# Two attention layers and two MLPs, forward and backward: the second turn's transposes, a row's transposition, the first V gradient blocks and the last stores in another order

## The chip, the cores and the metric

The kernel runs on one core of a Trainium2 chip. The metric is the time of one execution on the device, in microseconds (us); lower is better. The core has a matrix engine (PE, TensorE; its weight loads are shown apart as PEld), a vector engine (DVE), a scalar engine (ACT), a general engine (POOL, GpSimd) and a sync engine (SP), which here does nothing but issue DMA transfers. Sixteen DMA engines move the data between the chip's memory and the on-chip buffers. Each engine works through its own instructions in order; between engines there are semaphores, which the compiler's framework places from the reads and writes of each tile.

## The reference

A layer is a decode attention over a cache and a channel MLP, each behind a LayerNorm and with a residual; the same weights are used twice. The batch is 2, one token each, width 1024, 32 query heads over 4 key/value heads, 16,384 cached positions of 128 values, MLP width 3584, all in bf16.

```python
def _A_ref(x, k_cache, v_cache, wq, wo):
    q = (x @ wq).reshape(B, Sq, Hq, Dh).transpose(0, 2, 1, 3)
    k = jnp.repeat(k_cache, rep, axis=1)
    v = jnp.repeat(v_cache, rep, axis=1)
    p = _softmax(jnp.einsum("bhqd,bhkd->bhqk", q, k) * (Dh ** -0.5))
    o = jnp.einsum("bhqk,bhkd->bhqd", p, v)
    return o.transpose(0, 2, 1, 3).reshape(B, Sq, Hq * Dh) @ wo
def _B_ref(x, w1, b1, w2, b2):
    h = _gelu(_layernorm(x) @ w1 + b1)
    return h @ w2 + b2
x = x + _A_ref(_layernorm(x), ...); x = x + _B_ref(x, ...)   # layer 0
x = x + _A_ref(_layernorm(x), ...); x = x + _B_ref(x, ...)   # layer 1
```

What is returned is x and, by `jax.vjp` with a given gradient of x, the gradients of the input, the two caches (each 2 x 4 x 16384 x 128), Wq, Wo, W1, b1, W2 and b2: ten outputs, out_0 (x) to out_9.

## The kernel before, in words

Everything large passes through on-chip slots of 128 partitions x 4096 bf16 values (1 MB): sixteen slot tiles, and parts of tiles named e, ds and late at times when those are free. A quarter of one head's cache of one batch, a slab of Wq, Wo, W1 or W2, a transposed slab, or a block of a gradient on its way out, takes a slot (or half of one).

**The planner.** The code first lists pieces of work with `emit(fn, uses)` and only then runs them, in that very order (`Program`, L58 to L180). A piece names the chunks that it uses. `run` gives each chunk a slot as one comes free; the loads are issued on SP in the order of first use, so SP's queue is one line: a load that has to wait until its slot is free holds up every load behind it. `keep` looks for a chunk that is used again later: where the slots have room between the two uses, it stays and is not loaded again. The order on each engine is thus the order of the pieces, written by hand through lists, step numbers and the interleaving in the loops.

**The stages**, by the trace of before: attention forward of layer 0 to about 215 us, its MLP to 250, attention forward of layer 1 (`attn_fwd(1)`) to 413, the *second turn* to 448, attention backward of layer 1 (`attn_bwd(1)`) to 641, the turn to layer 0 to about 664, attention backward of layer 0 with all the weight and cache gradients beside it to 1097, and the last stores to 1107.9. A step of `attn_bwd` takes a quarter of a V chunk: a transpose on DVE (L537, 128 x 512 viewed as int32), eight products (L550), eight with K (L575), and small works hung on step numbers.

**The second turn** (L1447 to L1482). The residual xA of the second attention goes through a LayerNorm (`ln_fwd`, L623 to L645, called by `mlp_in`, L913): sums over partitions by PE (`part_sum`, L594) and short DVE operations that wait for each other. Then the products with W1 (`w1_fwd`, L854, matmuls at L862: eight chunks of W1, 28 products each), the gelu with its slope (L881 to L910), and, for the backward pass, the products with W1 transposed. For these each W1 chunk is turned on DVE (`turn_cols`, L470, instruction at L473): four column groups cg for each of eight chunks j, 32 turns. Chunks 0 to 3 make the first half and 4 to 7 the second; in each half, group cg of all four chunks lands in one turned chunk `w1t[half][cg]`, and there are eight of these. Each is read by 28 products (`turned_products`, L479, matmuls at L487). Besides, a slab of Wo is turned on PE and copied by ACT for the next pass (`wo_first_ops`, `turn_here`, L452 and L455; eight "wo turns" of eight 128 x 128 transposes). Before, four W1 turns lie behind `attn_fwd(1)`, twenty beside the W1 products with four wo turns, one in the middle of the gelu with the other four wo turns, and seven behind it; then all eight groups of products. `mlp_in_bwd` (L918) takes the products back through the LayerNorm; from there gA_all (L932) goes through Wo (L465), and attention backward starts.

**The row to an output** (`col_to_row`, L609). x and the input's gradient lie as columns, 128 partitions x 8 groups x 2 batches, in f32. Eight PE transposes (L617), 128 x 2 to 2 x 128 each, and two DVE copies (L618) make two rows of 1024 values in bf16, which a DMA (L619) stores. For out_0 this happens at step 30 of `attn_bwd(1)` (L1507), in a half slot, and the DMA is issued by POOL; for out_1 near the end, by SP.

**The gradients of the caches** (`kv_outputs`, L1197). For each group pos of `attn_bwd(0)`, four chunks c and both w (1: V, 0: K) fill a block of 1 MB with eight units (L1261 products of 512 columns, copied out by `cast_out`, L276 on ACT or L279 on DVE). With `fine` (L1234), the units take the two halves of the block one after the other, and each half is stored as soon as it is full (L1267 to L1269); without, one store of 1 MB by POOL follows the eighth unit (L1271). Before, `fine` holds for the last group's K blocks from c = 2 on.

**The end** (L1158 to L1161 and `pieces_rows`, L1335). What is left behind the last step is a list `todo`; `parts` are the pieces that end in out_1's row, `kv_units` the last cache units, `units` the last of a weight gradient, out_4, whose eight stores of 256 KB (L1349) SP issues.

Of the kernel before, what the change touches and what calls it, by code (L numbers as in the profile page):

```python
# [182 lines left out]
def kernel(  # L183
# [24 lines left out]
    nc = tc.nc  # L208
# [400 lines left out]
    def col_to_row(colT, dram_out, queue=None, kind="half"):  # L609
        c = P.chunk(kind=kind)  # L610

        def f():
            row = c.ap[0:2, 0:D]
            for j0 in range(0, DJ, 4):
                ps = ob()[0:2, :].rearrange("p (a b) -> p a b", a=4)
                for j in range(4):
                    PE.transpose(ps[:, j, :], colT[:, j0 + j, :], identf[:])  # L617
                V.tensor_copy(out=row[:, j0 * 128:(j0 + 4) * 128], in_=flat(ps))  # L618
            (queue or GP).dma_start(dram_out, row)  # L619

        return f, [c]

    def ln_fwd(xT, name, twice=False):  # L623
        s1 = small.tile([128, 2], F32, name="ln_s1")
        V.tensor_reduce(out=s1[:], in_=xT.rearrange("p j b -> p b j"), axis=AX.X, op=ALU.add)
        ps = part_sum(s1[:], 2)
        negmu = small.tile([128, 2], F32, name="ln_negmu")
        V.tensor_scalar(out=negmu[:], in0=ps, scalar1=-1.0 / D, scalar2=None, op0=ALU.mult)
        xc = wrk.tile([128, DJ, 2], F32, name="ln_xc")
        V.tensor_tensor(out=xc[:], in0=xT, in1=bcast_j(negmu[:], DJ), op=ALU.add)  # L630
        sq = wrk.tile([128, DJ, 2], F32, name="ln_sq")
        V.tensor_tensor(out=sq[:], in0=xc[:], in1=xc[:], op=ALU.mult)
        s2 = small.tile([128, 2], F32, name="ln_s2")
        V.tensor_reduce(out=s2[:], in_=sq[:].rearrange("p j b -> p b j"), axis=AX.X, op=ALU.add)
        ps2 = part_sum(s2[:], 2)
        vpe = small.tile([128, 2], F32, name="ln_vpe")
        V.tensor_scalar(out=vpe[:], in0=ps2, scalar1=1.0 / D, scalar2=LN_EPS, op0=ALU.mult, op1=ALU.add)
        if twice:
            V.scalar_tensor_tensor(out=vpe[:], in0=vpe[:], scalar=LN_EPS, in1=vpe[:], op0=ALU.mult, op1=ALU.add)
            V.tensor_scalar(out=vpe[:], in0=vpe[:], scalar1=-LN_EPS, scalar2=None, op0=ALU.add)  # L640
        rstd = vec.tile([128, 2], F32, name=name + "_rstd")
        GP.tensor_tensor(out=rstd[:], in0=vpe[:], in1=neghalf[:], op=ALU.pow)  # L642
        y = vec.tile([128, DJ, 2], F32, name=name + "_y")
        V.tensor_tensor(out=y[:], in0=xc[:], in1=bcast_j(rstd[:], DJ), op=ALU.mult)
        return y, rstd  # L645
# [264 lines left out]
        V.tensor_tensor(out=h_all[:, :, 2 * l:2 * l + 2], in0=sg[:], in1=hpre[:], op=ALU.mult)  # L910
        return slope() if dh is None else None

    def mlp_in(l, xT):  # L913
        y, r = ln_fwd(xT[:], f"m{l}", twice=True)
        V.tensor_copy(out=m_all[:, :, 2 * l:2 * l + 2], in_=y[:])
        saved[f"m{l}"] = (y, r)

# [109 lines left out]
    def attn_bwd(l, order, gT, wo_first, outputs=None, mark=None, extra=None):  # L1027
# [127 lines left out]
        if l == 1:  # L1155
            todo = tail + parts
        else:
            rows, kv_units, units = outputs(s, True)  # L1158
            todo = ev.pop(s) + kv_units[0:4] + rows + kv_units[4:6] + tail[0:4] + kv_units[6:8] + tail[4:] + kv_units[8:10]
            todo += parts[0:1] + units[0:4] + parts[1:2] + units[4:8] + parts[2:3] + kv_units[10:13] + parts[3:]  # L1160
            todo += kv_units[13:] + units[8:]  # L1161
        for b in todo:
            emit(*b)
        assert not ev and not wb and not pend and not extra, (ev, wb, extra)
# [32 lines left out]
    def kv_outputs(pos, g):  # L1197
# [30 lines left out]
        for c, w in [(c, w) for c in range(NCH) for w in (1, 0)]:  # L1228
            at_ = base + 4 * c + 4 * (pos == 0) if w == 1 else base + 14 + 4 * c
            if w == 0 and pos == G - 1:  # L1230
                at_ = (124, 127, N_END + 1, N_END + 2)[c]
            stg = P.chunk(kind="full")
            hold = {}
            fine = w == 0 and pos == G - 1 and c > 1  # L1234

            def turn(c=c, w=w, hold=hold):
                st["tp"] += 1
                tp = tpb[st["tp"] % 2][:].bitcast(BF16)[:, 0:512].rearrange("p (a b) -> p a b", b=128)
                for bi in range(4):
                    for l in range(2):  # L1240
                        src = d_of(l, pos, g) if w == 0 else e_of(l, g)
                        PE.transpose(tp[64 * l:64 * l + 64, bi, :],  # L1242
                                     src[:, 4 * c + bi].rearrange("p h b -> p (h b)"), ident[:])
                st["blk"] += 1
                blk = Bt[st["blk"] % 3]
                src = tp.rearrange("p a (j t) -> p a j t", j=4)
                dst = blk[:].rearrange("p j (a t) -> p a j t", a=4)
                if st["act"] + 0.36 <= st["dve"] + 0.4:
                    S.copy(out=dst.bitcast(I32), in_=src.bitcast(I32))
                    load_of("act", 0.36)  # L1250
                else:
                    V.tensor_copy(out=dst, in_=src)
                    dve(0.4)
                hold["blk"] = blk

            res.append((min(at_ - 2, N_END - 1), turn, ()))
            for u in range(8):
                def unit(c=c, w=w, u=u, hold=hold, stg=stg, fine=fine):
                    ps = ob()
                    j, hf = (u % 4, u // 4) if fine else (u // 2, u % 2)  # L1260
                    PE.matmul(ps, lhsT=hold["blk"][:, j, :],  # L1261
                              rhs=flat(qm(w)[:, hf * 4:hf * 4 + 4, :]), start=True, stop=True)
                    cast_out(stg.ap.rearrange("p (s j q d) -> p s q j d", j=4, q=2, d=128)[
                        :, hf * 2:hf * 2 + 2, :, j], ps.rearrange("p (s q d) -> p s q d", q=2, d=128))
                    if fine:
                        if j == 3:
                            (nc.sync if w == 0 else GP).dma_start(  # L1267
                                (dKv if w == 0 else dVv)[g, :, c * 32 + hf * 16:c * 32 + hf * 16 + 16, :],
                                stg.ap[:, hf * 2048:hf * 2048 + 2048].rearrange("p (t d) -> p t d", d=128))  # L1269
                    elif u == 7:  # L1270
                        GP.dma_start((dKv if w == 0 else dVv)[g, :, c * 32:(c + 1) * 32, :],  # L1271
                                     stg.ap.rearrange("p (t d) -> p t d", d=128))
                res.append((at_ + (u // 4 if pos or w == 0 else u // 3), unit, [stg, qc]))
# [61 lines left out]
    def pieces_rows(out_ap, n_in, n_out, c0=0, fine=False):  # L1335
# [6 lines left out]
        for j0, rb, cb, cn in parts:  # L1342
            units = [(j0 + j, c0 + cb + c, 512, j * cn + c) for j in range(rb) for c in range(0, cn, 512)]

            def store(ap, n, j0=j0, rb=rb, cb=cb, cn=cn, end=len(units) - 1):
                if fine:
                    if n % 2 == 1:
                        j = n // 2
                        nc.sync.dma_start(out_ap[(j0 + j) * 128:(j0 + j + 1) * 128, c0:c0 + cn], ap[:, j * cn:(j + 1) * cn])  # L1349
                elif n == end:  # L1350
                    GP.dma_start(out_ap[j0 * 128:(j0 + rb) * 128, c0 + cb:c0 + cb + cn].rearrange("(j p) n -> p j n", p=128),
                                 ap[:, 0:rb * cn].rearrange("p (j n) -> p j n", j=rb))
# [94 lines left out]
    ws1 = ld_w1()  # L1447
    w1t = [[P.chunk() for _ in range(4)] for _ in range(2)]

    def w1_turn(j, cgs=range(4)):  # L1450
        return [turn_cols(ws1[j], j % 4, w1t[j // 4][cg], cg) for cg in cgs]

    xA1 = attn_fwd(1, down, lambda: xM0, mark("e1"), w1_turn(0), tw[5][1] + tw[6][0] + tw[6][1] + [(dh_last_, ())])
    emit(lambda: mlp_in(1, xA1))
    hps1, w1_ops = w1_fwd(1, ws1)
    dm_1 = quads(at_sb0(224, 16))
    vh1, spread_h1 = spread(lambda: dh_all[:, :, 2:4], FJ, "vh")
    ws_o, wo_turns1, wo_prods = wo_first_ops(1, up[0] % HKV)
    for j in range(DJ):
        for b in w1_ops[j] + (w1_turn(j) if 1 <= j < 6 else []) + wo_turns1[2 * j - 10:2 * j - 8] * (j in (5, 6)):  # L1460
            emit(*b)

    def turn_round():

        def dh(nslope):
            V.tensor_tensor(out=dh_all[:, :, 2:4], in0=nslope[:], in1=dh_last[:], op=ALU.mult)
            spread_h1()

        gelu(1, hps1, dh, lambda: [fn() for fn, _ in w1_turn(6, (0,)) + wo_turns1[4:]])

    emit(turn_round, [ws1[6], w1t[1][0]] + ws_o)
    for cg in range(4):
        for b in (w1_turn(6, (cg,)) if cg else []) + w1_turn(7, (cg,)):
            emit(*b)
    for h in range(2):
        for cg in range(4):
            for b in turned_products(lambda h=h: dm_1[:, h], w1t[h][cg], 14 * cg, 14, vh1, cg == 0, cg == 3):
                emit(*b)
    def g3_():
        saved["g3"] = mlp_in_bwd(1, lambda dm: unquad(dm[:].rearrange("p (c j) b -> p c j b", j=4), dm_1), gT4)  # L1480

# [156 lines left out]
```

## Time and profile before

| what | value |
|---|---|
| three runs, median (lowest to highest) | 1110.71 us (1108.69 to 1111.01) |
| the profiled execution: time, span of its instructions | 1109.68 us, 1107.9 us |
| PE, PEld, DVE, ACT, POOL busy | 810.2, 608.8, 761.4, 492.3, 178.5 us |
| mean granted PE clock | 0.929 |
| moved by DMA, mean rate | 450.03 MB, 406 GB/s |
| loads of V, of K (1 MB each) | 98, 105 |

All times in the profile count from the start of the span. The page gives the busy time of each engine, then the span in 40 equal slices with a digit for the busy share of each engine in tenths, the PE clock as granted, the share of the DMA engines and the rate. Groups of instructions are named by line, engine, operation and tile (out<-in). The timeline gives the start, the length, and the number of like instructions in a run ("x7"), whose ends may overlap; brackets tell how long the engine stood idle before and what released it. "SPq" and "POOLq" are the DMA issues of those engines. The waits list, for each line, what its engine waited for: total, times, longest.

### The profile page before, as it was taken

The numbers are of one execution on the slowest core, as the hardware profiler recorded it, in microseconds if no ns is written. First come the engines' busy times: TensorE is split into PE (matmuls) and PEld (weight loads), VectorE is DVE, ScalarE is ACT, GpSimd is POOL, SyncE is SP. The second block draws the span as 40 slices with busy tenths as digits, with TensorE's granted clock in tenths as the row PEclk, the third lists the DMA queues.
The fourth block names the chain that finished last, engine by engine and source line by source line (L and its number), as shares of the span: only waits on it lengthen the run. The fifth ranks groups of instructions, "written<-read, shape, count | busy, mean of one in ns | idle before, by whom it ended". The sixth has DMA issues, their size and how long they took to land. (4 is left out here: it accounts for less than half of the span.)

```text
span 1107.9 us, 34190 instructions
## 1 busy us (share of the span) xinstructions
PE 810.2 (73%) x14677; PEld 608.8 (55%) x14689; DVE 761.4 (69%) x1474; ACT 492.3 (44%) x1133; POOL 178.5 (16%) x571
## 2 busy tenths in 40 slices
PE   5664666457888647888678668878886987598795
PEld 4554565456777547777677565444443444344453
DVE  5864665169888627665646475979776896598984
ACT  0322223102233222235444326777675776477874
POOL 1000000001000000111111101433332332233430
PEclk9999999999999999999878657989996998799998
DMA  9999999999999998999999989999999999999996
GB/s 375 420 423 421 421 426 421 395 403 399 418 422 422 421 421 328 409 417 421 420 421 421 417 326 406 369 381 423 420 419 425 423 420 422 425 412 420 410 423 259
DMA packets 98312, 450.03 MB, mean 406 GB/s; under 512 B 7624, under 2 KB 11734, under 8 KB 59632
## 3 DMA queue, kind: packets, MB, share of 16 engines
q1 hardware_dynamic: 81232, 353.41, 78.4%
q0 software_dynamic: 16928, 94.43, 20.7%
q8 instruction: 115, 1.88, 0.6%
q14 instruction: 37, 0.30, 0.1%
HBM read 349.20 MB, written 98.62 MB: 404 GB/s over the span
## 5 line engine op out<-in xcount | busy, mean ns | idle before, releaser
L537 DVE STREAM_TRANSPOSE kT<-slot 128x512 int32<-128x512 int32 x420 | 283.2, 694 | 109.8 <-PE sc L550 89.5
L550 PE MATMUL sc<-qbd,kT 128*128 128x32 bf16 x4096 | 262.9, 223 | 11.0 <-DVE kT L537 9.7
L550 PEld LDWEIGHTS <-kT 128*128 128x128 bf16 x4096 | 209.3, 115 | 63.7 <-issue 33.6
L575 PEld LDWEIGHTS <-slot 128*128 128x128 bf16 x3520 | 144.0, 103 | 108.6 <-issue 45.0
L575 PE MATMUL sb<-xt,slot 128*128 128x8 bf16 x3520 | 161.3, 177 | 51.1 <-DMA slot<-in_A_v_cache_dram 24.5
L276 ACT CAST slot<-sc 128x512 bf16<-128x512 f32 x293 | 166.5, 594 | 57.1 <-PE sc L1321 32.6
L1261 PE MATMUL sc<-slot,late 128*128 128x512 bf16 x345 | 128.8, 393 | 19.0 <-DVE slot L279 6.5
L279 DVE CAST slot<-sc 128x512 bf16<-128x512 f32 x170 | 113.7, 677 | 25.1 <-PE sc L1261 13.4
L763 ACT ACTIVATE e<-sc 128x512 bf16<-128x512 f32 x32 | 19.0, 597 | 235.9 <-DVE sc L760 168.3
L276 ACT CAST slot<-sb 128x512 bf16<-128x512 f32 x139 | 82.4, 593 | 38.8 <-PE sb L1321 16.9
L455 ACT COPY slot<-tp 128x512 int32<-128x512 int32 x88 | 50.2, 586 | 105.5 <-PE tp L452 105.2
L452 PE MATMUL tp<-ident,slot 128*128 128x128 bf16 x768 | 71.3, 255 | 11.9 <-DMA slot<-in_A_wq_dram 6.2
L585 ACT COPY xt<-e 32x128 int32<-32x128 int32 x256 | 75.6, 295 | 3.9
L1261 PEld LDWEIGHTS <-late 128*128 128x128 bf16 x512 | 44.5, 98 | 59.6 <-issue 46.1
L1261 PE MATMUL sb<-slot,late 128*128 128x512 bf16 x161 | 63.6, 395 | 11.7 <-DVE slot L279 6.5
L1321 PE MATMUL sc<-slot,late 128*128 128x512 bf16 x157 | 60.5, 404 | 12.3 <-DVE e L279 6.9
L437 DVE STREAM_TRANSPOSE slot<-slot 128x1024 int32<-128x1024 int32 (+1 forms) x48 | 55.3, 1177 | 16.8 <-DMA slot<-in_A_wo_dram 8.5
L452 PEld LDWEIGHTS <-slot 128*128 128x128 bf16 x768 | 57.9, 116 | 14.5 <-DMA slot<-in_A_wq_dram 6.7
L279 DVE CAST slot<-sb 128x512 bf16<-128x512 f32 x82 | 55.6, 678 | 9.2 <-PE sb L1321 3.9
L642 POOL TENSOR_TENSOR m_rstd<-ln_vpe,neghalf 128x2 f32<-128x2 f32 x2 | 1.4, 717 | 352.6 <-DVE ln_vpe L640 352.6
L585 POOL COPY xt<-late 32x64 int32<-32x64 int32 x240 | 55.2, 230 | 12.9 <-DVE late L1049 2.2
L585 POOL COPY xt<-ds 32x64 int32<-32x64 int32 x128 | 29.5, 231 | 158.6 <-DVE ds L1049 115.3
(300 smaller groups left out, 1098.7 us busy)
## 6 DMA issues: line engine op xcount, KB each, us to landing
slot<-in_A_k_cache_dram SPq DMA_DIRECT2D x105, 1024.0 KB, 17.5
slot<-in_A_v_cache_dram SPq DMA_DIRECT2D x98, 1024.0 KB, 18.0
out_dram<-slot POOLq DMA_DIRECT2D x55, 1024.0 KB, 14.4
slot<-in_A_wq_dram SPq DMA_DIRECT2D x25, 1024.0 KB, 16.1
slot<-in_A_wo_dram SPq DMA_DIRECT2D x25, 1024.0 KB, 19.7
slot<-in_B_w_dram SPq DMA_DIRECT2D x23, 896.0 KB, 15.8
out_dram<-slot POOLq DMA_DIRECT2D x40, 512.0 KB, 14.3
slot<-in_B_w_dram SPq DMA_DIRECT2D x12, 1024.0 KB, 13.5
```

The costliest lines, as they stand in the source:

```text
L276: S.copy(out=dst, in_=src)
L279: V.tensor_copy(out=dst, in_=src)
L437: V.transpose(out=t.ap[:, h * nw * 256:(h + 1) * nw * 256].bitcast(I32).rearrange("p (w j m) -> p w j m", j=4, m=32), in_=c.ap[:, 0:4 * nc ...
L452: PE.transpose(tp[:, j * 128:(j + 1) * 128], c.ap[:, off + j * 128:off + (j + 1) * 128], ident[:])
L455: S.copy(out=d.bitcast(I32), in_=tp.bitcast(I32))
L537: V.transpose(out=kT[:].bitcast(I32).rearrange("p (w j m) -> p w j m", w=4, j=4), in_=c.ap[:, (i % 4) * 1024:(i % 4 + 1) * 1024].bitcast(I ...
L550: PE.matmul(sc[:, a0:a0 + 4, :, 2 * (i % 4) + q], lhsT=kv[:, 2 * q + w, :, e], rhs=qbd[:, q_at(g), 2 * w + e], start=(w == 0 and e == 0), ...
L575: PE.matmul(acc, lhsT=c.ap[:, n * 128:(n + 1) * 128], rhs=xv[:, i // 4, t // 2, :, 2 * (i % 4) + t % 2], start=(fresh and i == 0 and t == ...
L585: (GP.tensor_copy if on[t % len(on)] == "g" else S.copy)(out=d[32 * t:32 * t + 32, c0:c0 + cn, j, :], in_=s[32 * j:32 * j + 32, c0:c0 + cn ...
L763: S.activation(out=e_of(l, g)[:, 8 * f:8 * f + 8].rearrange("p a h b -> p h a b"), in_=sc[f][:].rearrange("p h (a b) -> p h a b", b=8), fu ...
L1261: PE.matmul(ps, lhsT=hold["blk"][:, j, :], rhs=flat(qm(w)[:, hf * 4:hf * 4 + 4, :]), start=True, stop=True)
L1321: PE.matmul(ps, lhsT=hold[j // 4 * 4][:, j % 4, :], rhs=Y.ap[:, y_at + c0:y_at + c0 + cn], start=True, stop=True)
```

## The change

It has four parts.

1. `col_to_row` turns the columns with two transposes (128 x 8 to 8 x 128, one for each batch) and one copy, and the DMA stores sixteen pieces of 256 bytes in place of two rows of 2 KB.
2. The second turn: the 32 W1 turns stand in one list, the second half's by column group first. Two go behind `attn_fwd(1)`; three more, and the wo turns 0 to 2, go into the three waits of `ln_fwd` (the new argument `gaps`); twelve lie beside the W1 products, two after each chunk's; two with the wo turns 3 to 5 go into the gelu's middle; the other thirteen lie between the groups of products p0 and p1 in the order written in the diff, with the wo turns 6 and 7. Since a turned chunk of the second half is now first written after the products of an earlier one, the planner gives the second half's four turned chunks two slots in turn, so that a turn of group 2 writes where group 0 was read. On SP, the first three W2 loads get the slots of the first W1 chunks, and one V chunk is kept, not loaded again: 97 loads of V are left. The other loads stay in their order.
3. `fine` holds for the first group's V blocks too: eight POOL stores of 512 KB in place of four of 1 MB.
4. The end: out_4's stores of the first four row blocks are issued by POOL, the others by SP as before; two more cache units stand ahead of out_1's row.

```diff
     def col_to_row(colT, dram_out, queue=None, kind="half"):
         c = P.chunk(kind=kind)
         def f():
-            row = c.ap[0:2, 0:D]
-            for j0 in range(0, DJ, 4):
-                ps = ob()[0:2, :].rearrange("p (a b) -> p a b", a=4)
-                for j in range(4):
-                    PE.transpose(ps[:, j, :], colT[:, j0 + j, :], identf[:])
-                V.tensor_copy(out=row[:, j0 * 128:(j0 + 4) * 128], in_=flat(ps))
-            (queue or GP).dma_start(dram_out, row)
+            row = c.ap[0:DJ, 0:256].rearrange("p (b n) -> p b n", b=2)
+            ps = ob()[0:DJ, 0:256].rearrange("p (b n) -> p b n", b=2)
+            for b in range(2):
+                PE.transpose(ps[:, b, :], colT[:, :, b], identf[:])
+            V.tensor_copy(out=row, in_=ps)
+            (queue or GP).dma_start(dram_out.rearrange("b (j n) -> j b n", n=128), row)
...
-    def ln_fwd(xT, name, twice=False):
+    def ln_fwd(xT, name, twice=False, gaps=((), (), ())):
         ps = part_sum(s1[:], 2)
+        for fn in gaps[0]:
+            fn()
...
         ps2 = part_sum(s2[:], 2)
+        for fn in gaps[1]:
+            fn()
...
         GP.tensor_tensor(out=rstd[:], in0=vpe[:], in1=neghalf[:], op=ALU.pow)
+        for fn in gaps[2]:
+            fn()
...
-            todo += parts[0:1] + units[0:4] + parts[1:2] + units[4:8] + parts[2:3] + kv_units[10:13] + parts[3:]
-            todo += kv_units[13:] + units[8:]
+            todo += parts[0:1] + units[0:4] + parts[1:2] + units[4:8] + parts[2:3] + kv_units[10:15] + parts[3:]
+            todo += kv_units[15:] + units[8:]
...
-            fine = w == 0 and pos == G - 1 and c > 1
+            fine = w == 0 and pos == G - 1 and c > 1 or w == 1 and pos == 0
...
-                        nc.sync.dma_start(out_ap[...], ap[...])
+                        (GP if j0 < n_in // 256 else nc.sync).dma_start(out_ap[...], ap[...])
...
-    def w1_turn(j, cgs=range(4)):
-        return [turn_cols(ws1[j], j % 4, w1t[j // 4][cg], cg) for cg in cgs]
+    def w1_turn(h, j, cg):
+        return turn_cols(ws1[4 * h + j], j, w1t[h][cg], cg)
+    w1_turns = [w1_turn(0, j, cg) for j in range(4) for cg in range(4)]
+    w1_turns += [w1_turn(1, j, cg) for cg in range(4) for j in range(4)]
+    def both(ops):
+        return [fn for fn, _ in ops], [c for _, us in ops for c in us]
-    xA1 = attn_fwd(1, ..., w1_turn(0), ...)
-    emit(lambda: mlp_in(1, xA1))
+    xA1 = attn_fwd(1, ..., w1_turns[0:2], ...)
+    gaps = [w1_turns[2:3] + wo_turns1[0:1], w1_turns[3:4] + wo_turns1[1:3], w1_turns[4:5]]
+    emit(lambda: mlp_in(1, xA1, [both(ops)[0] for ops in gaps]), both(sum(gaps, []))[1])
     for j in range(DJ):
-        for b in w1_ops[j] + (w1_turn(j) if 1 <= j < 6 else []) + wo_turns1[2 * j - 10:2 * j - 8] * (j in (5, 6)):
+        for b in w1_ops[j] + (w1_turns[5 + 2 * j:7 + 2 * j] if j < 6 else []):
             emit(*b)
...
-        gelu(1, hps1, dh, lambda: [fn() for fn, _ in w1_turn(6, (0,)) + wo_turns1[4:]])
-    emit(turn_round, [ws1[6], w1t[1][0]] + ws_o)
-    for cg in range(4):
-        for b in (w1_turn(6, (cg,)) if cg else []) + w1_turn(7, (cg,)):
-            emit(*b)
-    for h in range(2):
-        for cg in range(4):
-            for b in turned_products(..., w1t[h][cg], 14 * cg, 14, vh1, cg == 0, cg == 3):
-                emit(*b)
+        gelu(1, hps1, dh, lambda: [fn() for fn in both(w1_turns[17:19] + wo_turns1[3:6])[0]])
+    emit(turn_round, both(w1_turns[17:19] + wo_turns1[3:6])[1])
+    p0, p1 = [[turned_products(..., w1t[h][cg], 14 * cg, 14, vh1, cg == 0, cg == 3)[0] for cg in range(4)]
+              for h in range(2)]
+    for b in (w1_turns[19:20] + p0[0:1] + w1_turns[20:24] + p0[1:4] + wo_turns1[6:7] + p1[0:1] + w1_turns[24:28] +
+              wo_turns1[7:8] + p1[1:2] + w1_turns[28:32] + p1[2:4]):
+        emit(*b)
```

More of the change, by code (lines that the diff above doesn't have):

```diff
@@ L911, in gelu, with mlp_in @@
         return slope() if dh is None else None
-    def mlp_in(l, xT):
-        y, r = ln_fwd(xT[:], f"m{l}", twice=True)
+    def mlp_in(l, xT, gaps=((), (), ())):
+        y, r = ln_fwd(xT[:], f"m{l}", twice=True, gaps=gaps)
         V.tensor_copy(out=m_all[:, :, 2 * l:2 * l + 2], in_=y[:])
@@ L1348, in store @@
                         j = n // 2
-                        nc.sync.dma_start(out_ap[(j0 + j) * 128:(j0 + j + 1) * 128, c0:c0 + cn], ap[:, j * cn:(j + 1) * cn])
+                        (GP if j0 < n_in // 256 else nc.sync).dma_start(out_ap[(j0 + j) * 128:(j0 + j + 1) * 128, c0:c0 + cn], ap[:, j * cn:(j + 1) * cn])
                 elif n == end:
@@ L1448 @@
     w1t = [[P.chunk() for _ in range(4)] for _ in range(2)]
-    def w1_turn(j, cgs=range(4)):
-        return [turn_cols(ws1[j], j % 4, w1t[j // 4][cg], cg) for cg in cgs]
-    xA1 = attn_fwd(1, down, lambda: xM0, mark("e1"), w1_turn(0), tw[5][1] + tw[6][0] + tw[6][1] + [(dh_last_, ())])
-    emit(lambda: mlp_in(1, xA1))
+    def w1_turn(h, j, cg):
[4 more added lines that the diff above has]
+        return [fn for fn, _ in ops], [c for _, us in ops for c in us]
+    xA1 = attn_fwd(1, down, lambda: xM0, mark("e1"), w1_turns[0:2], tw[5][1] + tw[6][0] + tw[6][1] + [(dh_last_, ())])
     hps1, w1_ops = w1_fwd(1, ws1)
@@ L1467, in dh @@
             spread_h1()
-        gelu(1, hps1, dh, lambda: [fn() for fn, _ in w1_turn(6, (0,)) + wo_turns1[4:]])
-    emit(turn_round, [ws1[6], w1t[1][0]] + ws_o)
-    for cg in range(4):
-        for b in (w1_turn(6, (cg,)) if cg else []) + w1_turn(7, (cg,)):
-            emit(*b)
-    for h in range(2):
-        for cg in range(4):
-            for b in turned_products(lambda h=h: dm_1[:, h], w1t[h][cg], 14 * cg, 14, vh1, cg == 0, cg == 3):
-                emit(*b)
+        gelu(1, hps1, dh, lambda: [fn() for fn in both(w1_turns[17:19] + wo_turns1[3:6])[0]])
+    emit(turn_round, both(w1_turns[17:19] + wo_turns1[3:6])[1])
+    p0, p1 = [[turned_products(lambda h=h: dm_1[:, h], w1t[h][cg], 14 * cg, 14, vh1, cg == 0, cg == 3)[0] for cg in range(4)]
+              for h in range(2)]
+    for b in (w1_turns[19:20] + p0[0:1] + w1_turns[20:24] + p0[1:4] + wo_turns1[6:7] + p1[0:1] + w1_turns[24:28] +
+              wo_turns1[7:8] + p1[1:2] + w1_turns[28:32] + p1[2:4]):
+        emit(*b)
     def g3_():
```

## The prediction

> **What bounds the kernel now.** I read the page's slices first: the DMA engines are the bound, and the time can change only where they are not full.
>
> ```profile
> DMA  9999999999999998999999989999999999999996
> GB/s 375 420 423 421 421 426 421 395 403 399 418 422 422 421 421 328 409 417 421 420 421 421 417 326 406 369 381 423 420 419 425 423 420 422 425 412 420 410 423 259
> ```
>
> A slice is 27.7 us. Full is some 420 GB/s; the hole at 328 (415 to 443 us) is the second turn, the last slice (259) the end. An edit elsewhere has to move DMA work to count. Next, the windows of the second turn (columns: stretch, its length, busy us of PE, PEld, DVE, ACT, POOL, then PEclk, DMA share, GB/s):
>
> ```profile
> 424.00:426.00 2.00, 2.00 (x43) 2.00 (x41) 1.91 (x4) 1.04 (x2) 0.00 (x0) 1.00 0.99 379
> 426.00:428.00 2.00, 2.00 (x42) 2.00 (x41) 2.00 (x5) 1.17 (x2) 0.00 (x0) 1.00 0.85 255
> ...
> 434.00:436.00 2.00, 2.00 (x81) 2.00 (x79) 2.00 (x5) 0.00 (x0) 0.00 (x0) 1.00 0.26 111
> 436.00:438.00 2.00, 2.00 (x81) 2.00 (x79) 1.37 (x3) 0.00 (x0) 0.00 (x0) 1.00 0.08 11
> 438.00:440.00 2.00, 1.71 (x64) 1.61 (x61) 0.22 (x2) 0.05 (x1) 0.00 (x0) 1.00 0.95 250
> ```
>
> The DMA stands nearly still at 434 to 438 because SP has nothing it may issue: its loads need slots that the W1 turns (L473, DVE) still read. Over 424 to 448 some 2.8 MB are missing against 420 GB/s: 6.6 us. Third, the timeline after the hole (start, length, engine, line):
>
> ```profile
> 487.85 1.04 PE L617 MATMUL sb<-identf,xM 128*2 128x128 f32 x4
> 488.68 1.01 PE L617 MATMUL sc<-identf,xM 128*2 128x128 f32 x4
> 490.71 0.62 POOL L619 DMA_DIRECT2D out_dram<-ds  x1 [7.23 <-DVE ds L618]
> 495.44 0.33 SPq L373 DMA_DIRECT2D ds<-in_A_v_cache_dram  x1
> ```
>
> This is what I weigh most. out_0's row stands in the slot ds, and the next V load goes there; SP issues in order, so every load behind it waits too. SP issues at 482.64 and next at 495.44; the waits by engine give it one line:
>
> ```profile
> SPq L373 <- DMA out_dram<-ds: 12.4, 1, 12.4
> ```
>
> Between 411 and 514 no compute engine waits for a load: the compute, not the DMA, sets when 490.71 comes.
>
> **The change part by part.** All is reckoned against the profiled execution: 1109.68 us, span 1107.9. The three runs' median, 1110.71, is 1.0 above it.
>
> *Second turn, DMA.* The moved W1 turns (five early ones, three of them in the LayerNorm's idle 0.75, 0.75 and 0.84 us at L628, L637, L644) free slots of ws1 by about 420, so the first three W2 loads need no longer be issued as late as 426.69 and 436.93. One V load of 1 MB falls away, its chunk being kept: 2.5 us at 420 GB/s. Of the 6.6 us hole I reckon 1 to 2.5 left, so the loads behind it lie 4 + 2.5 = **6.5 us earlier**.
>
> *Second turn, compute.* hpre (428.64) needs the last W1 load, which lands at 426.27 in the trace, plus 28 products at L862 (0.93): about 427.3. From there gelu, spread and the first dm group take what they take now, plus one turn: p0[0] ends near 433.7 (433.59 + 0.89 = 434.5 now). But the second half's turned chunks now share two slots, so turns wait for products (write after read), where four own slots made none. Row by row: a turn is 0.545 us (L473, 7 in 3.79), a group of 28 products 0.767 (L487, 196 in 5.37), a wo turn 0.93 (L452). p0[1..3] end at 436.0, wo6 at 436.9, p1[0] at 437.7; only then come the four turns of cg2 (2.2: 439.9), after p1[1] the four of cg3 (442.1), and p1[3] ends at 442.9 to 443.0, against 439.7 now. That is **3.3 us later** for the chain behind it (L517, the LayerNorm's backward, gA_all at 443.69, the first kT turn L537 at 448.07). Queued behind the waiting turns on DVE is only that chain. ACT's moved Exp (L891) is on no one's path.
>
> *Row to out_0.* col_to_row: eight f32 transposes (1.04 + 1.01 us of PE) and two copies (0.68 each) become two transposes and one copy of 8 x 256, so at most a quarter of the PE time (0.5) and half of one copy's columns (0.34). From 487.85 to the copies' end the row now takes 2.56 us (489.73 + 0.68 - 487.85), then 0.95 or less: some 1.6 us saved on the way to 490.71. The DMA of 16 pieces of 256 B has no row of its own: between 2 us (an idle queue) and the present 4.7 us from issue to landing (490.71 to 495.38), nearer 3 to 4.7, as the loads around it are fewer.
>
> *Sum at the gate.* Compute +3.3, row -1.6, store -1.7 to 0: SP goes on at 495.4 + (0 to 1.7), I take **+0.8**. From here SP's order is the same. The loads before the gate would by then have landed, so their 6.5 us lead ends as an empty DMA: before, too, the V load issued at 495.44 lands at 500.89, 5.45 after its issue, just as the W2 load from the idle queue (436.93 to 442.37, 5.44). So the lead is not passed on. After 514 PE waits 23 us and DVE 13 us for loads before 641, which swallows the compute's lateness.
>
> *Halves.* The first group's V gradient goes out as eight 512 KB stores for four of 1 MB: four more POOL issues (0.62 for one, by L619) and 4 KB packets. All those stores have landed by 721.6 now, and the hole there (720 to 724, 231 GB/s) follows POOL's own copies (L585, 716.08 to 720.42), not the stores. POOL is busy 16%. I take 0; -1 (the first half goes earlier) to +0.5.
>
> *End.* Four of eight 256 KB stores (L1349) go from SP to POOL, and out_1's row costs 1 us less.
>
> ```profile
> 1097.41 2.77 SPq L1349 DMA_DIRECT2D out_dram<-slot  x2
> 1100.37 0.97 SPq L1349 DMA_DIRECT2D out_dram<-ds  x2
> ```
>
> The last cast ends at 1097.22, yet SP issues until 1101.01, each store waiting for one of eight earlier ones. Freed of it, the last issue could come 3.3 us sooner. But the stores then land evenly, one every 0.63 us, from 1099.78 to 1106.57: of each store's sixteen parts fifteen land 3 to 11 us before the last, and the last is always of one engine, 7 to 12 us behind since 1030. A straggler with a backlog does not care which queue issued. I take -0.3; ends -3.3 and 0.
>
> Sum: 1109.68 + 0.8 + 0 - 0.3 = **1110.2**; with the bounds (gate -0.6 to +1.7, halves -1 to +0.5, end -0.5 to 0) 1108 to 1112.
>
> **A rule weighed.** Until 489.5 PE ran at half pace, from then at full, right behind the f32 transposes:
>
> ```profile
> 487.45 0.59 PE L550 MATMUL sc<-qbd,kT 128*128 128x32 bf16 x8
> 489.74 0.39 PE L550 MATMUL sc<-qbd,kT 128*128 128x32 bf16 x8
> ```
>
> (107 ns a 128-column transpose before, 56 after; the PEclk column shows 1.00 before 489.5, where no clock record stands.) By this row the transposes raise the clock, and the change takes them out. If nothing else raised it up to 641, the products (97 groups of eight, 0.20 longer) and wo/wq turns (some 72, 0.43 longer), each in the 58% of the time in which PE is now at full clock, cost 11 + 18 = 29 us, against 23 of PE's waits: +6. But PE goes back to 0.50 and up again several times at 510 to 640 with no f32 work there, so I hold it for unlikely. [...]
>
> **Rivals.**
> (a) *The lead carries through* (chance 0.18): if the gate opens some 6 us earlier, or out_0's store is not in SP's way, the 6.5 us stay: about **1103.5**. For: the DMA is the bound from 726 on, and 6.5 us of it are really saved. Against: the 12.4 us wait; compute sets it.
> (b) *The lanes bound the end* (0.17): issue 3.3 us sooner, landing 3.3 sooner: **1106.5**. For: the waits of SP at L1349 (4.3, 3 and 2.1 us). Against: the straggler's even pace.
> (c) *Slower: the products' wait goes through the gate* (0.15). The place is SP's wait at the ds slot; the price is the whole +3.3, if the store of small pieces lands as slowly as now and the row gains nothing, its transposes waiting behind PE's queue anyway: **1113**. It decides from the point where POOL's issue comes later than 492.9, 2.2 behind now.
> (d) *The clock stays at half* (0.08): +6, **1116**, decided if L550 still takes 0.59 at 510.
> That the change doesn't do what it says (the V load stays, or the hole) would leave the gate as it is: within my forecast.
>
> **How the numbers follow.** 0.2% (2.2 us) is about what a measurement of this kernel can tell from no change. My forecast, 1110.2, has 0.42. Faster 0.18 + 0.17 = 0.35 (a half of (a) with little lead left lies inside the range); slower 0.15 + 0.08 = 0.23 (c and d); same 0.42. The range leaves out the farther half of (a) and (d), 0.17: 1104.5 to 1114. The likeliest case alone: 1108 to 1112.
>
> **What would show it.** Right: the hole at 434 to 438 gone, 97 V loads, L517 at about 443, POOL's L619 at 492 to 493, a fall of GB/s at 488 to 498 that was not there, SP going on at 495 to 497, last landings at 0.63 us apart. Wrong: L517 before 440 (the turns don't wait as reckoned), L619 before 489 (the lead is kept), or a last store issue and landing both 3 us sooner.

## The result, and the profile after

The changed kernel takes 1108.12 us in the median of 22 runs (1106.67 to 1110.80), the kernel before 1110.35 us in 22 runs (1108.43 to 1113.30): a ratio of 0.9981, with a 95% interval of 0.9975 to 0.9987. That is 2.1 us, or 0.19%, less by the ratio (2.2 us between the medians): clear of no change, yet just within the 0.2% that I had called the same, and 2.1 us under the 1110.2 of the forecast. The profiled execution took 1108.56 us, its span 1106.8.

The page's slices of the changed kernel, for those shown of before:

```profile
DMA  9999999999999999999999989999999999999996
GB/s 373 420 423 421 422 425 421 398 381 406 417 423 420 422 420 381 414 371 417 419 422 422 416 324 412 348 400 423 420 421 425 424 419 421 423 391 420 415 422 267
```

The slice of the second turn (the sixteenth) has risen from 328 to 381 GB/s, that is by 1.5 MB or 3.5 us at 420; but the eighteenth (470 to 498 us) has fallen from 417 to 371, by 1.3 MB or 3.0 us. The windows show both (columns as in the prediction):

```profile
432.00:434.00 2.00, 1.17 (x44) 1.17 (x44) 1.70 (x4) 0.00 (x0) 0.00 (x0) 0.50 0.69 269
434.00:436.00 2.00, 2.00 (x77) 2.00 (x75) 1.98 (x4) 0.00 (x0) 0.00 (x0) 0.50 0.77 223
436.00:438.00 2.00, 2.00 (x42) 2.00 (x41) 0.41 (x1) 0.59 (x1) 0.00 (x0) 0.50 0.89 353
...
490.00:492.00 2.00, 2.00 (x69) 2.00 (x66) 2.00 (x4) 0.59 (x1) 0.68 (x1) 1.00 0.89 340
492.00:494.00 2.00, 1.16 (x35) 1.06 (x31) 1.97 (x5) 1.09 (x4) 0.46 (x2) 1.00 0.28 104
494.00:496.00 2.00, 1.84 (x47) 1.73 (x48) 2.00 (x5) 1.85 (x7) 1.40 (x7) 1.00 0.58 139
```

At 434 to 438 the DMA moved 111 and 11 GB/s before, 223 and 353 now. At 490 to 496 it was all but full before:

```profile
490.00:492.00 2.00, 2.00 (x63) 1.92 (x60) 2.00 (x4) 0.59 (x1) 0.62 (x1) 1.00 1.07 450
492.00:494.00 2.00, 1.17 (x35) 1.07 (x31) 1.97 (x4) 1.01 (x3) 0.36 (x2) 1.00 0.99 417
494.00:496.00 2.00, 1.76 (x44) 1.65 (x45) 2.00 (x5) 1.82 (x8) 1.49 (x7) 1.00 0.99 388
```

Now there is a hole of 3.2 us (80, 316 and 281 GB/s short of 420, for 2 us each). SP stands there at out_0's slot, as the timeline and the waits of the changed kernel say:

```profile
490.60 0.68 POOL L618 DMA_DIRECT2D out_dram<-ds  x1 [5.72 <-DVE ds L617]
493.81 0.33 SPq L373 DMA_DIRECT2D ds<-in_A_v_cache_dram  x1
```

```profile
SPq L373 <- DMA out_dram<-ds: 9.4, 1, 9.4
```

So more than half of what the second turn gains is given back 55 us later. How much of it, the landings of the loads tell. They are matched one to one in the traces, from the start up to the load that is gone and from the end behind it. Executions differ by up to 2.2 us before the changes can act, so each shift is taken against the last eight W1 loads (411 to 426 us); shifts are medians of the loads in a stretch. In the changed kernel the loads land 5.2 us sooner at 455 to 492, and from 510 to 770 only 2.3 to 2.4 us sooner. That is the gain that the medians show; towards the end of this one execution 0.8 us of it is left.

### The profile page after: what moved, and what is told of

Read it like the earlier page. It is cut to its first block, busy times and chain, and to the rows that moved or that the text cites. A ratio compares the mean times of both kernels' runs of the same rounds, so it can differ in the third digit from the quotient of the medians.

```text
span 1106.8 us, 34173 instructions
## 1 busy us (share of the span) xinstructions
PE 807.9 (73%) x14665; PEld 606.4 (55%) x14677; DVE 760.3 (69%) x1472; ACT 493.1 (45%) x1133; POOL 183.8 (17%) x579
## 5 line engine op out<-in xcount | busy, mean ns | idle before, releaser
L550 PE MATMUL sc<-qbd,kT 128*128 128x32 bf16 x4096 | 261.8, 222 | 11.1 <-DVE kT L537 10.2
L550 PEld LDWEIGHTS <-kT 128*128 128x128 bf16 x4096 | 208.8, 115 | 60.1 <-issue 29.4
L276 ACT CAST slot<-sc 128x512 bf16<-128x512 f32 x281 | 160.7, 594 | 60.0 <-PE sc L1266 23.4
L1266 PE MATMUL sc<-slot,late 128*128 128x512 bf16 x343 | 129.2, 397 | 27.2 <-DVE slot L279 14.2
L276 ACT CAST slot<-sb 128x512 bf16<-128x512 f32 x151 | 89.5, 593 | 35.3 <-PE sb L1326 23.9
L1266 PEld LDWEIGHTS <-late 128*128 128x128 bf16 x512 | 44.8, 99 | 61.5 <-issue 48.7
L1266 PE MATMUL sb<-slot,late 128*128 128x512 bf16 x163 | 64.9, 398 | 7.9 <-DVE slot L279 2.4
```

Of the source, the lines that this page charges most:

```text
L276: S.copy(out=dst, in_=src)
L550: PE.matmul(sc[:, a0:a0 + 4, :, 2 * (i % 4) + q], lhsT=kv[:, 2 * q + w, :, e], rhs=qbd[:, q_at(g), 2 * w + e], start=(w == 0 and e == 0), ...
L1266: PE.matmul(ps, lhsT=hold["blk"][:, j, :], rhs=flat(qm(w)[:, hf * 4:hf * 4 + 4, :]), start=True, stop=True)
```

## The experiments

The gate theory: what the second turn wins is a lead of the DMA; it is used up where SP waits for out_0's store in the slot ds, and what is left behind that gate is the gain. "Gate" stands here for that wait of SP. Rivals: the lead or the row gains by itself, the halves or the end hold a part, or other waits matter more. Ratios are to the kernel before, run on the same chip. "Shift" is that of the loads as above: before the gate (455 to 492 us), behind it (510 to 560), at 745 to 770.

| kernel | ratio (95%) | shift before the gate, behind it, at 750 |
|---|---|---|
| changed kernel | 0.9981 (0.9975 to 0.9987) | -5.2, -2.4, -2.3 |
| row alone | 1.0004 (0.9994 to 1.0014) | 0.0, +0.1, -1.1 |
| second turn alone | 1.0000 (0.9988 to 1.0012) | -5.2, +0.1, -0.1 |
| row and second turn | 0.9984 (0.9975 to 0.9993) | -5.1, -1.4, -1.6 |
| halves and end alone | 1.0000 (0.9991 to 1.0008) | +0.1, +0.1, -0.1 |
| changed, row in its own tile | 0.9958 (0.9944 to 0.9972) | -5.0, -4.5, -5.4 |
| row in its own tile, old second turn | 1.0005 (0.9997 to 1.0014) | +0.2, +0.2, -0.4 |
| row, second turn, own tile; no halves, no end | 0.9946 (0.9933 to 0.9960) | -5.2, -4.4, -4.4 |
| changed, third slot for the turns | 1.0016 (1.0006 to 1.0025) | -4.9, -2.0, +3.0 |
| third slot and own tile | 0.9999 (0.9989 to 1.0009) | -3.3, -3.3, +1.4 |
| third slot, no halves | 1.0016 (1.0006 to 1.0027) | -4.7, -1.9, -0.3 |

A shift is of one execution, and worth about 1 us (the row alone shows -1.1 at 750, and no gain). In three executions (changed with its own tile, third slot and own tile, third slot without halves) the eight W1 loads themselves move by 1.0 to 1.6 us against each other, so that the shifts of these three rows are uncertain by about as much. The second turn is tested as one edit: how much of its lead comes from the V load that falls away, and how much from the hole that is filled, no run separates.

**The parts.** The row alone takes only the change of `col_to_row`:

```diff
-            row = c.ap[0:2, 0:D]
...
+            row = c.ap[0:DJ, 0:256].rearrange("p (b n) -> p b n", b=2)
```

> Before with the new row (col_to_row) alone. Gate theory: SP goes on some 1.6 to 3 us sooner than 495.4, but before's DMA was not empty at that place (388 and 378 GB/s at 494 to 498, together some 0.4 us lost), so only that comes back: -0.4 us, ratio 0.9993 to 1.0000. Rival, the row by itself is what the change gains: -1.6 to -3, ratio 0.9973 to 0.9985.

Measured 1.0004: no gain, as the gate theory has it. POOL's issue came at 490.30 in an execution that was 1.6 us late by then, so 2.0 us sooner than before; but the DMA had work (the two loads queued last landed at 497.57 and 500.17, behind the store's 495.17):

```profile
492.00:494.00 2.00, 1.68 (x54) 1.58 (x50) 1.97 (x4) 0.80 (x2) 0.17 (x1) 1.00 1.03 436
494.00:496.00 2.00, 1.57 (x38) 1.48 (x39) 2.00 (x4) 1.81 (x9) 1.66 (x8) 1.00 1.00 414
```

The second turn alone takes `gaps`, the list of the turns and their order, and leaves the row, the halves and the end as before:

```diff
+    gaps = [w1_turns[2:3] + wo_turns1[0:1], w1_turns[3:4] + wo_turns1[1:3], w1_turns[4:5]]
...
+    for b in (w1_turns[19:20] + p0[0:1] + w1_turns[20:24] + p0[1:4] + wo_turns1[6:7] + p1[0:1] + w1_turns[24:28] +
+              wo_turns1[7:8] + p1[1:2] + w1_turns[28:32] + p1[2:4]):
```

> Before with the new second turn alone, the row as it was. Gate theory: POOL's issue comes at 490.6 + 1.5 = 492.1, the store lands some 3 to 4.7 us later, SP goes on at 495.2 to 496.8 and the DMA's lead is lost before it: -0.2 to +1.4 us, ratio 0.9998 to 1.0012. Rival, the lead or the V load that is not made carries through: -2.2 or more, ratio 0.998 or less.

Measured 1.0000. The lead of 5.2 us is there, and all of it goes at the gate. POOL's issue came at 493.86, not at the 492.1 that I had expected. The windows of this kernel, and its timeline:

```profile
492.00:494.00 2.00, 2.00 (x51) 1.83 (x49) 1.71 (x3) 0.35 (x1) 0.14 (x1) 0.95 0.18 70
494.00:496.00 2.00, 2.00 (x60) 1.82 (x56) 1.97 (x5) 0.51 (x2) 0.48 (x1) 1.00 0.01 2
496.00:498.00 2.00, 0.97 (x31) 0.79 (x28) 2.00 (x4) 1.52 (x6) 1.04 (x5) 1.00 0.75 201
```

```profile
493.86 0.62 POOL L619 DMA_DIRECT2D out_dram<-ds  x1 [7.01 <-DVE ds L618]
495.57 0.33 SPq L373 DMA_DIRECT2D ds<-in_A_v_cache_dram  x1
```

The last load that SP had issued landed at 493.45 by the trace, so the row came too late by itself, and the store had an empty DMA: it landed 1.7 us behind its issue.

Both together, without halves and end (their lines as before):

> Row and second turn together, without the halves and without the end's edits. Gate theory: all of the gain, -2.1 us, ratio 0.998. Rival, the halves or the end hold a part: -1.5 us or less, ratio over 0.9986.

Measured 0.9984, the changed kernel's within the intervals. Two edits that are worth nothing apart are worth 1.8 us together (the interval, 0.9975 to 0.9993, lies clear of 1, and just overlaps that of the second turn alone). And the rest, with the two cache units of `todo`:

```diff
...
-            fine = w == 0 and pos == G - 1 and c > 1
+            fine = w == 0 and pos == G - 1 and c > 1 or w == 1 and pos == 0
...
+                        (GP if j0 < n_in // 256 else nc.sync).dma_start(out_ap[...], ap[...])
```

> Before with the halves and the end's edits alone. My theory: the stores of the first group were no bound and the end goes by the one late DMA engine: 0, ratio 0.9993 to 1.0005. Rival, SP's waits bound the end: last issue some 4 us sooner and 1 to 3.3 us gained, ratio 0.997 to 0.999.

Measured 1.0000: the halves and the end give nothing.

**The gate taken away.** out_0's row stands in a small tile of an earlier stage, dead by then, in place of the load slot (`col_to_row` gets the argument `own` for it):

```diff
-    extra[30] = [col_to_row(xM1, out_0.rearrange("b s d -> (b s) d"), kind="load")]
+    extra[30] = [col_to_row(xM1, out_0.rearrange("b s d -> (b s) d"), own=lambda: vec.tile([128, 4, 4, 16], BF16, name="vg")[:].rearrange("p a b n -> p (a b n)"))]
```

> The changed kernel, but out_0's row stands in a small tile of its own (that of an earlier stage, dead by then) and no longer in the load slot ds, so that no load waits for its store. Gate theory: SP issues the V load some 9 us sooner, the hole at 490 to 496 (340, 104, 139 GB/s: 3.2 us at 420) is gone, some 3 us less than the changed kernel: ratio to before 0.995 to 0.996. Rival, the loads behind it wait for slots that the compute frees anyway: nothing more than the changed kernel, ratio 0.998.

Measured 0.9958, or 4.7 us less than before. SP issues the V load at 489.49, 4.3 us sooner than in the changed kernel (I had expected some 9), the hole is gone, and 4.5 of the 5.0 us pass on. Its windows:

```profile
490.00:492.00 2.00, 2.00 (x38) 1.86 (x39) 1.42 (x3) 0.00 (x0) 0.07 (x1) 0.50 1.06 415
492.00:494.00 2.00, 2.00 (x49) 2.00 (x47) 1.49 (x4) 0.58 (x1) 0.61 (x1) 0.56 1.04 420
494.00:496.00 2.00, 1.45 (x45) 1.35 (x41) 1.97 (x5) 1.10 (x4) 0.46 (x2) 1.00 1.02 424
```

The counter-test is the new row in a tile of its own (the edit just shown) with the old second turn:

> Before with the new row in a tile of its own, the second turn as before. Gate theory: without the lead the DMA has work at 490 to 498 anyway, so an open gate gives as little as the new row alone: ratio 0.9985 to 1.0005. Rival, the wait at the slot costs its 2.5 us by itself, whatever lies before it: ratio 0.998 or less.

Measured 1.0005: without a lead the open gate is worth nothing. And the same without halves and end, with the new second turn:

> Row, second turn and the row's own tile, without the halves and without the end's edits. Gate theory: the open gate alone makes the gain, ratio 0.995 to 0.9965 as the own tile in the changed kernel had (0.9958). Rival, the halves matter once the stores of the first group stand closer to earlier loads: ratio over 0.997.

Measured 0.9946 (0.9933 to 0.9960), the median 1104.99 us, the best of all. Its interval overlaps that of the kernel with halves and end, so it shows no help from these behind an open gate, and no loss either.

**The turns' wait.** The turns of group 2 stand ahead of p1[0], and the planner gives them a third slot:

```diff
-    for b in (... + p0[1:4] + wo_turns1[6:7] + p1[0:1] + w1_turns[24:28] + wo_turns1[7:8] + p1[1:2] + w1_turns[28:32] + p1[2:4]):
+    for b in (... + p0[1:4] + w1_turns[24:28] + wo_turns1[6:7] + p1[0:1] + w1_turns[28:32] + wo_turns1[7:8] + p1[1:4]):
```

> The changed kernel, but the turns of column group 2 stand ahead of wo turn 6 and p1[0], so that the planner gives them a third slot and they wait for no product; group 3 still waits for p1[0]. p1[3] should end at 441.3 in place of 442.9. Gate theory: POOL's issue and the gate come 1.5 us sooner, 1.5 us less than the changed kernel: ratio 0.9967. Rival, the compute's lateness is made up before the gate: ratio 0.998 as the changed kernel.

> Both: the third slot and the row in a tile of its own. Gate theory: with the gate open the DMA is full from 440 to 500, so a compute that is 1.5 us sooner gives nothing: as the own tile alone, ratio 0.9955 to 0.996. Rival, the loads behind 448 wait for slots that the compute frees, and come 1.5 us sooner: ratio 0.9945.

Measured 1.0016 and 0.9999. Both theories miss: 3.9 and 4.5 us slower than without the third slot. The products did end sooner (uq, L517, at 442.06 in an execution 1.0 us late, so 1.6 us sooner than in the changed kernel, which was 0.2 late), but the gate gave no more: the last queued load landed at 494.63 and out_0's store at 494.79, so that SP went on at 494.85 in this execution, in the changed kernel at 493.81: with the two offsets taken off, no sooner. The loss comes much later, in the first group of `attn_bwd(0)`; windows of the third slot kernel:

```profile
704.00:708.00 4.00, 4.00 (x32) 2.00 (x31) 2.23 (x4) 2.34 (x5) 0.53 (x1) 0.50 0.45 188
708.00:712.00 4.00, 4.00 (x28) 1.88 (x25) 2.61 (x4) 2.15 (x5) 0.00 (x0) 0.50 0.34 137
712.00:716.00 4.00, 3.95 (x37) 1.85 (x36) 3.67 (x7) 3.33 (x7) 1.62 (x3) 0.88 0.65 170
```

and its longest wait of SP there (684 to 732 us):

```profile
SPq L373 <- PE sc L1266: 21.3, 2, 21.0
```

In the changed kernel the same windows have 342, 330 and 352 GB/s, and the longest such wait for L1266 is 6.4 us:

```profile
704.00:708.00 4.00, 3.87 (x28) 1.64 (x28) 3.55 (x6) 3.23 (x6) 1.26 (x2) 1.00 0.86 342
708.00:712.00 4.00, 3.75 (x45) 2.04 (x43) 3.75 (x7) 3.30 (x6) 0.54 (x2) 1.00 1.04 330
```

The planner hands out slots in order, so that a load which takes another slot can pass this on, load by load, to 700 us. The traces leave slot numbers out; what they show is the times of issue: a Wo load is issued at 684.47 and not at 690.90, a V load at 692.17 and not at 700.77, and the next K load at 713.38 and not at 707.33. The stores of the first group land later behind the early loads (the one issued at 690.76 after 8.8 us; at 689.48 in the changed kernel after 5.8), and ACT and DVE wait 1.8 and 1.4 us for one of them at 700 to 702. If the halves had brought it about, it would go without them:

> The third slot without the halves (the first group's V blocks in four stores of 1 MB). The third slot lost 4.7 us at 704 to 716, where Wo and V loads had been issued 6 to 9 us sooner and the stores of the first group landed later. If the halves bring that about: ratio 0.998. If the loads' new places alone do: 1.0016 as before, or more.

Measured 1.0016: not the halves. Here the shift is -1.9 behind the gate, -0.3 at 750 and +3.3 at 1000 to 1085, so that the loss is spread over more places. PE's clock has a part in it too. In all three kernels with the third slot it falls at 700 to 712 (to 0.50 in the first two of the windows above, in which PE is busy throughout; to 0.50 at 700 to 708 with the own tile; to 0.77 to 0.80 at 704 to 712 without the halves), and in the kernel before, the changed kernel, row and turn, and the own tile it is 1.00 all through; SP then waits for PE. Whether the late stores bring the clock down is not shown. That the loads' new places stand at the start of the loss is what the traces speak for; I have not shown it by a kernel that alters these alone.

## Why the prediction was right, and where its sum was off

*What bounds.* Right: the second turn's 6.6 us were not the gain, and where the DMA's lead went is out_0's slot. That was the step on which the forecast stood, and the kernel with the row's own tile shows it: 0.9981 becomes 0.9958 by that alone. But the forecast let all of the lead go there, and in the changed kernel 2.4 of 5.2 us pass.

*Second turn, DMA.* The lead was 5.2 us, not 6.5. Over 424 to 448 us the rate was 308 GB/s before, which is 6.4 us short of 420 (I had said 6.6), and is 369 now, 2.9 us short, where I had reckoned with 1 to 2.5 left. The K load behind the four W2 loads waited until 434.49 for a slot that the products p0 still read (8.4 us on PE at L487).

*Second turn, compute.* Right: uq (L517) at 442.93 for the forecast 443, the first kT turn at 451.27 in place of 448.07, +3.2 for +3.3. (Two short waits for W1 loads, 0.7 us at L473 and 0.2 at L862, do stand between 411 and 514 before; both lie ahead of 427.) The turns wait for products as reckoned; the timeline of DVE:

```profile
433.75 2.23 DVE L473 STREAM_TRANSPOSE ds<-slot 128x448 int32<-128x448 int32 x4 [0.30 <-PE sb L487]
437.59 2.22 DVE L473 STREAM_TRANSPOSE slot<-slot 128x448 int32<-128x448 int32 x4 [1.61 <-PE sb L487]
439.74 2.18 DVE L473 STREAM_TRANSPOSE ds<-slot 128x448 int32<-128x448 int32 x4
```

*Row.* Right: from 489.24 to the copy's end at 490.30, 1.06 us in place of 2.56, 1.5 saved for 1.6.

*The sum at the gate* is the term that was mis-sized, and its sign was wrong: +0.8, measured -2.3 for the loads of the changed kernel and -1.4 for those of row and turn. Three things were off.

First, POOL's issue came at 490.60, 1.8 us before the 492.4 that follow from the forecast's steps. The 3.2 us of lateness had shrunk to 1.4 at the row. In this execution PE had its full clock, by the clock records, at 469.3 to 472.7 and 476.1 to 482.9, before only from 489.5; the timelines have L550 so, the changed kernel first, before second:

```profile
478.05 0.39 PE L550 MATMUL sc<-qbd,kT 128*128 128x32 bf16 x8
479.05 0.59 PE L550 MATMUL sc<-qbd,kT 128*128 128x32 bf16 x8
```

That this made up the 1.8 us is argued from these records, not shown. With row and turn alone PE was at half until 492.8 but for 468.9 to 472.3 and 482.6 to 486.0, and the issue came at 492.18, with the kernel's own offset of -0.5 at 492.7, as the forecast's steps have it.

Second, the store. I had it land 3 to 4.7 us behind its issue. In the changed kernel it took 3.15 us and landed at 493.75, just behind the last queued load (493.60); with row and turn it took 1.69 us and landed at 493.87 (load 493.70); with the second turn alone, no load being left, 1.66 us, where I had put 2 for an idle queue. Before and in the row alone, where loads were queued for longer, it took 4.68 and 4.87 us and landed ahead of the last two of them (before at 495.38; the loads at 495.91 and 498.46). So in these runs it landed either about 4.8 us after its issue or right behind the last queued load, whichever came first, and never sooner than 1.7 us after its issue. Where there is a lead, the gate therefore opens at the later of two times, the last queued load's landing and POOL's issue plus 1.7; the compute's lateness counts only where it passes the loads, as in the second turn alone. That also says why the part of the change that has the least to do with the DMA, the row, decides whether there is a gain: without it POOL's issue comes at 493.86, behind the loads.

Third, I read the V load of before (issued 495.44, landed 500.89) as one from an empty queue, so that SP's delay would be the whole shift. But the queue was not empty before: the load ahead landed at 498.46, and the V load 2.43 us behind it, at full pace (1 MB in 2.43 us is 431 GB/s). In the changed kernel the V load, issued at 493.81, landed at 498.60, 5.0 us behind the load ahead of it (493.60): that is what the gate costs there. The loads behind the gate thus lie 2.3 us sooner, 1.6 by SP's issue and 0.65 by the shorter time to landing (4.80 us for 5.45).

The forecast was no change, and its range held; but by the sum it held with some luck. Its errors at the gate, some 3 us, all went one way, and the gain of 0.19% stayed within the 0.2% by a hair.

*Halves, end.* Right, 0 for both. In the changed kernel SP's last store is issued at 1096.43, 4.6 us sooner than before, and the last landing, 1105.63, is only 0.9 sooner; the last ones of SP still land one every 0.63 us (1103.73, 1104.36, 1105.00, 1105.63). Rival (b) falls with it: SP's lanes did not bound the end. With halves and end alone the last issue is at 1098.70, 2.3 us sooner, and the last landing at 1107.63, no sooner than before. That the last part is always of the same engine can't be read from the traces, which don't name it. What they show is one of the sixteen engines' worth of work: a DMA share of 0.06 to 0.07 at 23 to 27 GB/s (1103 to 1106 before, 1101 to 1105 in the changed kernel); the pace, a sixteenth of 256 KB in 0.63 us or 26 GB/s, is a sixteenth of 420 GB/s.

*The rule weighed.* Rival (d) falls: without the run of eight f32 transposes PE went to full clock all the same, at 489.8 in the changed kernel and at 491.8 to 493.8 in the kernels of the row alone, row and turn, and own tile. What raised it stays open. Two f32 transposes (L616) are left in the new row. In the kernel before, the changed one and six others (row alone, second turn alone, row and turn, and the three with an own tile and no third slot) a stretch of full clock begins 0.5 to 3.2 us after the row's first f32 transpose, wherever that stands (486.6 to 491.4). This may be the transposes or other work of the same step; what is shown is that eight are not needed, and that the clock also rose where no f32 transpose stood near (469.3 and 476.1 in the changed kernel, and seven times at 510 to 640 before, at 513.4, 533.9, 547.5, 574.8, 591.9, 622.6 and 629.5, where the only f32 work on PE is the short sums of L594 at 528.6 and 582.4).

*Rivals (a) and (c).* (a) is what the own tile brings about: 4.7 us of the 6.2 that it named. (c) had the right place, but its price is bounded by the loads: even the second turn alone was not slower (1.0000).

## What to carry to other kernels

A lead in a queue is worth what gets past the next place where the queue runs dry; look for that place before summing up what an edit saves, and mend the gate first: a row of 4 KB in a load slot cost 2.6 us here. Edits that are worth nothing one by one can be worth something together, where one makes the lead and the other opens the gate sooner, so test them in pairs. Where a planner hands out slots in order, an edit of one stage can change who waits for whom 250 us later, and lose more than it gains.

## What the runs showed that I had not expected

A small store issued among loads is not quick because it is small: 4 KB landed 4.87 us after its issue with loads queued (row alone), and 1.7 us after it with none (second turn alone). The clock of PE differs between executions of nearly the same instructions: between 450 and 486 us the changed kernel had two stretches of full clock (469.3 to 472.7 and 476.1 to 482.9), the one with the third slot none (0.50 in every window of 2 us). The changed kernel and that of row and turn run the same work up to out_0's store, and still POOL's issue of it lay 2.3 us apart in the two (each against its own offset). Thanks to the gate, little of that is left in the time.
